# Values spread over partition groups by SBUF-to-SBUF DMA, Q and K transposed straight from staging, attention steps regrouped by PE tile mode

## The chip, the cores and the metric

The kernel runs on one core of one Trainium2 chip. The metric is device time in microseconds (us) of one execution. Most executions of one kernel lie within about 1 %; some fall into a slower state, with a lower granted TensorE clock. A ratio is the mean time of one kernel's fast runs over the mean time of the other's fast runs of the same rounds, so it is not quite the ratio of the medians that are quoted beside it.

Engines are named as the profile names them: PE is TensorE (matmul), DVE is VectorE, ACT is ScalarE, POOL is GpSimd, SP is SyncE, which issues DMAs. SBUF is the memory on the chip that the engines work on, HBM the large memory beside it. The *mode* of a matmul is the shape in which it uses TensorE's array; the profile prints it in each line (64\*128, 128\*128, 128\*64).

## The reference

Block-sparse attention (4 batches, 8 heads, 768 rows, 64 columns per head), followed by a two-layer network with exact GELU over the 3072 rows of 512.

```python
block, n_blocks, n_rand = 32, 24, 3
mask  = |block(i) - block(j)| <= 1                   # own block and both neighbours
mask |= block(i) in (0, 23) or block(j) in (0, 23)   # the first and last block, as rows and as columns
mask |= block(j) in sampled_blocks[block(i)]         # three drawn blocks for each query block
attn = softmax(where(mask, q @ k.T / sqrt(64), -1e9))
x = (attn @ v), heads side by side: [3072, 512]
out = gelu(x @ w_in) @ w_out                         # w_in [512, 2048], w_out [2048, 512]
```

Three kinds of score blocks follow from the mask. A query tile of 128 rows has "own" keys (itself and its neighbours, masked after the exponential), "global" keys (blocks 0 and 23) and "sampled" keys (four slots of 32: three drawn blocks and one more, gathered by GpSimd). The query rows of blocks 0 and 23 see every key: these are the "dense" steps.

## The kernel before

A batch is handled in two halves of 384 rows, a half in four head pairs. For each half there is a *hidden stage* (the `w_in` matmuls and GELU, with the next half's transposes and gathers filled in between) and then an *attention stage* (the next half's attention, with the `w_out` matmuls of this half filled in between). TensorE runs everything in program order.

```python
# Values: cast, to HBM, and back 16 times, so that partition group s holds the blocks rotated by s
def prep_v(b, v_st):
    dve.tensor_copy(v_pj, v_st.rearrange("p h (j d) -> p j h d", d=D))
    sp.dma_start(out=v_dram[b]..., in_=v_pj...)
def spread_v(b):
    for c in range(4):
        for s in range(4):
            i = 6 * ((c - s) % 4)
            sp.dma_start(out=v_rep[32 * s:32 * s + 32, i:i + 6, :], in_=v_dram[b]...[c])
def natural_v(b, eng):            # copies for the own and the global keys; ScalarE for batch 0
    copy(v_nat[b % 2][:, :, :, 0:D], v_rep[:, 0:NT, :]...)
    ...
# Q and K: a permuted copy, six transposes, one eviction
def transpose_qk(b, hp, which, pair, eng, st):
    pm = permute(pair, eng)       # one copy of 128x768, on VectorE in batches 1 to 3
    ps = mm_pool.tile([P, NT, P], BF16, tag="mm", name="ps")
    for j in range(NT):
        pe.transpose(ps[:, j, :], pm[:, j, :, :].rearrange("p h d -> p (h d)"), ident)
    dve.tensor_copy(dst..., ps...)
# Scores: two steps per pair, each with 64-row matmuls followed by 128-row ones
def scores_own(b, hb, hp, st):
    for m in range(MH):
        for h in range(2):
            pe.matmul(s1[:, h, ...], lhsT=kt[64 h : 64 h + 64, c], rhs=qt[64 h : 64 h + 64, c])
    for m in range(2):
        pe.matmul(s1[:, m, HALF:HALF + P], lhsT=gl, rhs=qt[:, ...])
    act.activation(pt[:, 0], s1, AF.Exp, scale=scale)
def scores_sampled(b, hb, hp, st):
    ... 22 matmuls of 64x32 from kg, then 2 of 128x64 from gl, then one Exp
...
def attention_steps(b, hb, st): ...   # own, sampled, late weighted, dense, ...
merge(attention_steps(...), output_steps(...))   # spreads the output pairs evenly between the steps
```

Every operation goes through one helper that keeps program order, so nearly all instructions carry its line (L52 before, L54 after); the lines of the profile are told apart by their tiles. Names: `s`, `sd` are scores, `pt`, `pd` their exponentials, `og`, `od` weighted sums, `psx`, `xT` the transposed attention output, `hp` the hidden layer, `g` its GELU, `op` the output layer, `tq`, `tk` transposed Q and K, `kg`, `v_gat` gathered keys and values.

The softmax here doesn't subtract the row's maximum and nothing guards it: scores larger than these inputs give would overflow.

## Time and profile before

The time before was 368.53 us (median of 3 runs, 367.51 to 368.89). The profile that came with it fell into a slow run (377.65 us). The kernel was profiled once more beside the experiments (369.58 us, mean granted clock 0.976; a single run, so of unknown state, but at the time of the fast ones). That profile is used below. These are its span, the busy time of TensorE and TensorE's busy tenths in 40 slices:

```profile
span 367.8 us, 8258 instructions
...
PE 280.2 (76%) x3632; PEld 159.7 (43%) x3632; DVE 158.3 (43%) x358; ACT 153.0 (42%) x173; POOL 107.9 (29%) x119
...
PE   0340038899977759886996999867978898999995
```

Each digit stands for 9.2 us. The first seven are a start in which TensorE mostly waits; after that it is busy, with dips. TensorE's waits from its first `w_in` matmul (69.4 us) to the end, from the list of waits (total us, times, longest):

```profile
PE ps L52 <- DVE pm L52: 21.3, 20, 2.6
PE og L52 <- POOL v_gat L52: 4.1, 2, 2.5
PE sd L52 <- ACT pt L52: 3.9, 3, 1.3
PE hp L52 <- DVE xT L52: 3.6, 4, 1.1
PE s L52 <- ACT pt L52: 3.0, 4, 0.9
PE psx L52 <- DVE x L52: 0.9, 4, 0.2
```

They sum to 36.8 us (0.7 of it in front of that first matmul), and 21.3 of them are for the permuted copy `pm`. In the timeline of TensorE (start, duration, what, and the idle time before it) this looks so:

```profile
105.94 0.51 PE L52 MATMUL ps<-ident,pm 128*128 128x128 bf16 x6 [1.91 <-DVE pm L52]
106.29 1.46 PE L52 MATMUL hp<-xT,w_in_sb 128*128 128x384 bf16 x8
108.04 0.51 PE L52 MATMUL ps<-ident,pm 128*128 128x128 bf16 x6 [0.29 <-DVE pm L52]
```

One set of six transposes takes 0.35 us (105.94 to 106.29), but TensorE waits before it. The start is bound by the values. In the timeline of ScalarE, the copy of the values stands in front of the first exponential and waits for the DMAs back from HBM; in that of TensorE, the first dense scores wait for that exponential:

```profile
44.06 2.75 ACT L52 COPY v_nat<-v_rep 128x3072 bf16<-128x3072 bf16 x1 [20.61 <-DMA v_rep<-v_dram]
```

```profile
49.50 0.50 PE L52 MATMUL sd<-tq,tk 64*128 64x64 bf16 x12 [22.56 <-ACT pt L52]
...
54.80 0.41 PE L52 MATMUL og<-v_gat,pt 128*32 128x65 bf16 x14 [2.06 <-POOL v_gat L52]
...
69.37 1.12 PE L52 MATMUL hp<-xT,w_in_sb 128*128 128x384 bf16 x3 [0.73 <-DVE xT L52]
```

The last line is where the start ends. I cut the span there, and after that at each change between hidden and attention work in TensorE's timeline:

| part of the span (us) | before |
|---|---|
| start, to the first `w_in` matmul | 69.4 |
| 8 hidden stages | 120.4, of which waits 21.3 |
| 7 attention stages with output matmuls | 163.7, of which waits 14.8 |
| last output stage | 14.4 |
| span | 367.8 |

### The profile page before, as it was taken

To read this page: it belongs to the slowest core of one execution; us is meant where nothing else is said; L and a number is where in the kernel's file an instruction comes from. 1 tells how busy PE (TensorE), PEld (TensorE's weight loads), DVE (VectorE), ACT (ScalarE), POOL (GpSimd) and SP (SyncE) were. 2 spreads that over 40 slices of the span, in tenths; PEclk is the share of its full clock that TensorE was granted. 3 is DMA by queue.
4 is the path that set the end of the run, shared out by engine and by line. 5 is a ranking of instruction groups with operands and counts; after the bars stand their busy time and mean duration, and the time that the engine had idled before them with its cause. 6 is when DMAs were issued, how large, how long until landed. Compare 5 with 4: busy or idle time off the path is not lost. (4 is left out here: it accounts for less than half of the span.)

```text
span 375.9 us, 8258 instructions
## 1 busy us (share of the span) xinstructions
PE 284.4 (76%) x3632; PEld 161.5 (43%) x3632; DVE 164.7 (44%) x358; ACT 153.3 (41%) x173; POOL 108.4 (29%) x119
## 2 busy tenths in 40 slices
PE   0340058699966859786896989876997899999995
PEld 0230046454543425443453545543554455545552
DVE  4298035513467625726446255535564045014201
ACT  2410366066321714223650575244523843475330
POOL 8331467430012374320244553100342531000000
PEclk9999999599998979969999999999999999999999
DMA  5979909978900029359201490179010000001102
GB/s 186 241 187 258 197 7 186 203 157 184 222 30 2 0 36 214 81 171 211 50 30 58 61 192 32 77 197 202 32 38 20 2 30 31 30 2 41 46 0 84
DMA packets 34419, 37.82 MB, mean 101 GB/s; under 512 B 2000, under 2 KB 30800, under 8 KB 34384
## 3 DMA queue, kind: packets, MB, share of 16 engines
q1 hardware_dynamic: 18576, 23.67, 24.0%
q0 software_dynamic: 14720, 12.06, 20.7%
q10 hardware_dynamic: 1088, 1.57, 1.1%
q8 instruction: 28, 0.46, 0.5%
q14 instruction: 7, 0.06, 0.1%
HBM read 39.92 MB, written 9.44 MB: 131 GB/s over the span
## 5 line engine op out<-in xcount | busy, mean ns | idle before, releaser
L52 PE MATMUL op<-w_out_sb,g 128*128 128x512 bf16 x384 | 106.7, 385 | 0.0
L52 ACT ACTIVATE g<-hp 128x768 bf16<-128x768 f32 x64 | 51.9, 811 | 123.5 <-PE hp L52 123.5
L52 PE MATMUL hp<-xT,w_in_sb 128*128 128x384 bf16 x512 | 92.7, 340 | 7.5 <-DVE xT L52 7.5
L52 POOL INDIRECT_COPY kg<-tk,idx_k 128x704 f32 x32 | 40.8, 1276 | 109.4 <-issue 72.6
L52 PEld LDWEIGHTS <-w_in_sb 128*128 128x128 bf16 x512 | 51.3, 102 | 43.3 <-issue 13.9
L52 DVE TENSOR_TENSOR pt<-pt,mask_x 128x768 bf16<-128x768 bf16 x32 | 28.8, 899 | 85.0 <-ACT pt L52 85.0
L52 PE MATMUL ps<-ident,pm 128*128 128x128 bf16 x192 | 18.8, 245 | 41.1 <-DVE pm L52 21.8
L52 POOL INDIRECT_COPY v_gat_201<-v_rep,idx_v 128x1024 f32 (+1 forms) x12 | 19.7, 1640 | 69.1 <-issue 35.6
L52 PEld LDWEIGHTS <-g 128*128 128x128 bf16 x384 | 29.2, 98 | 16.9
L52 PEld LDWEIGHTS <-pm 128*128 128x128 bf16 x192 | 13.4, 109 | 49.6 <-DVE pm L52 28.6
L52 PEld LDWEIGHTS <-pt 128*32 128x32 bf16 (+2 forms) x1024 | 26.2, 100 | 18.5 <-issue 6.8
L52 PEld LDWEIGHTS <-tk 64*128 64x128 bf16 x384 | 10.7, 100 | 46.3 <-issue 45.6
L52 DVE COPY os<-op 128x512 f32<-128x512 f32 x24 | 16.5, 688 | 23.2 <-PE op L52 23.1
L52 POOL INDIRECT_COPY v_gat_202<-v_rep,idx_v 128x1024 f32 (+1 forms) x12 | 19.6, 1636 | 21.4 <-issue 8.7
L52 PE MATMUL sd<-tq,tk 64*128 64x64 bf16 x192 | 6.2, 202 | 25.8 <-ACT pt L52 25.8
L52 DVE COPY tk<-ps 128x768 bf16<-128x768 bf16 x16 | 15.3, 956 | 23.7 <-PE ps L52 23.7
L52 ACT ACT_TABLE_LOAD x16 | 20.5, 1283 | 6.7 <-issue 4.8
L52 ACT ACTIVATE pd<-sd 128x768 bf16<-128x768 f32 x16 | 13.0, 813 | 19.4 <-PE sd L52 19.4
L52 DVE COPY tq<-ps 128x768 bf16<-128x768 bf16 x16 | 15.3, 958 | 7.4 <-PE ps L52 7.2
L52 DVE TENSOR_TENSOR x<-og,rc 128x384 bf16<-128x384 f32 x32 | 17.8, 557 | 1.1
L52 DVE RECIPROCAL rc<-og 128x6 f32<-128x6 f32 x32 | 6.2, 194 | 25.1 <-PE og L52 25.0
L52 PEld LDWEIGHTS <-kg 64*128 64x128 bf16 x704 | 11.2, 94 | 12.9 <-issue 10.3
(321 smaller groups left out, 304.7 us busy)
## 6 DMA issues: line engine op xcount, KB each, us to landing
out_dram<-os SPq DMA_DIRECT2D x24, 256.0 KB, 2.0
st_v<-in_v_dram POOLq DMA_DIRECT2D x4, 768.0 KB, 15.2
v_rep<-v_dram_205 SPq DMA_DIRECT2D x16, 192.0 KB, 8.5
v_rep<-v_dram_206 SPq DMA_DIRECT2D x16, 192.0 KB, 6.5
v_rep<-v_dram_207 SPq DMA_DIRECT2D x16, 192.0 KB, 7.0
v_rep<-v_dram_208 SPq DMA_DIRECT2D x16, 192.0 KB, 6.1
st<-in_k_dram POOLq DMA_DIRECT2D x6, 384.0 KB, 7.3
st<-in_q_dram POOLq DMA_DIRECT2D x6, 384.0 KB, 9.5
```

The costliest lines, as they stand in the source:

```text
L52: return self._tc.keep_in_program_order(f(*args, **kwargs))
```

## The change

Its intent is to take work and waits off TensorE's path, in three parts:

1. **Values.** They are read in their natural layout as float32 (runs of 256 bytes), cast once into a buffer `v_flat`, and rotated over the four groups of 32 partitions by six SBUF-to-SBUF DMAs. The trip through HBM, the copy to `v_nat` and the waiting ScalarE copy are gone.
2. **Transposes.** The permuted copy `pm` is gone. Each head is transposed from the staging tile itself (in batch 0 from a plain bf16 cast of it): 12 transposes of 64 columns, in column-tiled mode, instead of 6 of 128.
3. **Attention by tile mode.** The 64-row score matmuls of a pair (own and sampled) run as one group and the 128-row ones after them. The dense steps use zero-padded 128x128 operands (`qgl`), so they too run in the full mode. Output matmuls come in larger blocks, with the counts written into the schedule.

It also reorders the start: index arithmetic is shared between VectorE and GpSimd, and the memsets move to VectorE.

```diff
 # values
-    def prep_v / spread_v / natural_v ...
+    def own_v(b, st_v, i, eng):
+        cast(eng, v_own[b % 2][:, 3 * i:3 * i + 3, :, 0:D], st_v[:, 3 * i:3 * i + 3])
+    def rotate_v(b, r):
+        for lo, hi, src in ((0, P - 32 * r, 32 * r), (P - 32 * r, P, 0)):
+            sp.dma_start(out=v_all[lo:hi, NT * r:NT * r + NT], in_=v_own[b % 2][src:src + hi - lo])
+    def global_v(b, s, eng): ...          # four small copies to vgl, from the rotated groups
 # transposes
-        pm = permute(pair, eng)
...
-            pe.transpose(ps[:, j, :], pm[:, j, :, :].rearrange("p h d -> p (h d)"), ident)
+            for h in range(2):
+                pe.transpose(ps[64 * h:64 * h + 64, j, :], pair[:, h, j * D:j * D + D], ident)
 # scores: both buffers at once, by mode
+        s1 = sc_pool.tile(...)
+        s2 = sc_pool.tile(...)
+        ... 6 own and 22 sampled matmuls of 64 rows, then
+        for m, o in enumerate((s1[:, 0, HALF:HALF + P], s1[:, 1, HALF:HALF + P], s2[:, 0, NR_Q:NR_Q + P])):
+            pe.matmul(o, lhsT=gl, rhs=qt[:, q0 + m * P:q0 + m * P + P], start=True, stop=True)
+        ... three activations instead of two
 # schedule: (step, output parts after it)
+            steps = [(S_(0), 3), (D_(0), 2)]
+            for hp in range(1, NPAIR):
+                steps += [(S_(hp), 0), (E_(hp - 1), 0), (W_(hp - 1), 2), (D_(hp), 2)]
...
 # start
     for hp in range(NPAIR):
         ...
         if hp == 0:
+            load_w_in(0)
+            value_columns()
+            value_indices(0, dve)
+            mark_valid(0)
+            clear_rest()                  # VectorE memsets
+        elif hp == 1:
+            load_w_in(1)
+            own_v(0, first_v, 0, dve)
+            own_v(0, first_v, 1, act)
+            for r in range(1, 4):
+                rotate_v(0, r)
+    for s in range(4):
+        global_v(0, s, dve)
+    for c in range(len(VCH)):
+        gather_v(0, 0, c)
...
+    value_indices(1, pool)
```

## The prediction

> **What bounds the kernel now.** Two stages. (1) Start: in the timeline TensorE has its first w_in matmul only at 71.7 us. It waits there for Values: they go to HBM (issued 19.4 us) and come back as 16 spread DMAs (issued 22.7 to 35.0); ScalarE, in program order, waits 20.0 us for them (list of waits) before its first exponential at 47.8, and the first weighted sum ends after the third gather, at about 54.5. (2) From 71.7 on TensorE is the limit: the sum over windows has it busy 252 of the last 296 us. Its idle time there is mostly waits in the stages with Q/K transposes: the list of waits has 21.8 us on the permuted copy `pm` (19 waits, longest 2.9), about 8 on evictions, 6.2 on gathered values, 4 on exponentials. The profiled run was a slow one (377.65 against a median of 368.53; windows show granted clock 0.74 to 0.93 between 60 and 180 us), so I cost in differences.
>
> **Mode changes.** "TensorEngine Tiling (Array Packing)", Key Properties, says that changing the tiling mode drains the array. The trace agrees: two output matmuls take 0.43 us when the next is of the same mode, 0.53 when it is not, so about 0.10 us per change.
>
> **Costs per head pair, from starts in the timeline at full clock, switches included.** Own plus sampled scores 1.04 us now; 6 + 22 in one mode, then 3 global: estimate 0.80. Weighted sum 0.86, without the 128x64 part 0.75. Dense scores 0.38 -> 0.34; dense weighted 0.60 -> 0.34. First halves gain 4 x 0.65, second halves 4 x 0.35. Over the seven halves beside output matmuls about 14 us, all on TensorE, so critical.
>
> **Transposes.** Without the permute the 21.8 us of `pm` waits go. They become 12 transposes of 64 columns in a 128x64 mode instead of 6 of 128: if the two column halves overlap, 24 cost 0.7 + 0.2 us; if not, about 1.5. Before 0.68. Loss 2 to 10 us over 12 pairs, I take 5. VectorE has two evictions of 0.96 us per pair left, so some waits return; two pairs stand back to back in batches 1 and 2. I estimate 38 us of idle becoming 14.
>
> **Start.** First loads of 4.7 MB landed at 18 us. Values are now read as 256-byte runs; "DMA: Bandwidth & Descriptors", Specifications, wants 512 B for line rate (no run here shows that yet). Estimate: Values land at 20 to 24 us, last Q/K at 25 to 28, rotation (2.4 MB, 6336 B pieces, 8 us at the 235 ns per 6144 B seen) at about 34, three gathers at 3.5 us to 45. ScalarE no longer waits, so scores of pairs 0 and 1 are done by then. First w_in matmul at about 60 instead of 72: gain 12 us, uncertain by 6.
>
> **Sum.** -14 (modes) + 5 (transposes) - 24 (waits) - 12 (start) = -45: **322 us**, 8 in 10 between 308 and 342. Faster by over 2%: 0.93; within 2%: 0.05; slower: 0.02.
>
> **What would show it.** `pm` waits gone, waits of `ps` under 10 us; TensorE idle after the first w_in matmul under 20 us; first w_in matmul at 55 to 65 us; ScalarE's long wait for `v_rep` gone; 24 transposes within 1.0 us; output pairs at 0.43 more often; dense weighted 0.34.
>
> **What would make it wrong.** 256-byte value loads or rotation far slower than estimated, so the start gains nothing (+10); column-tiled transposes that do not overlap (+5); TensorE waiting for exponentials since both score buffers are taken at once (third exponential per pair), or for VectorE with the f32 casts; output stores stuck behind value loads on the same queue; GpSimd copies slowing VectorE.

## More of the kernel before

A wait is counted in the stage in which it falls. The waits for `xT` in front of the first `w_in` matmul of later hidden stages (2.8 us) therefore belong to the attention stages. The text on record for experiment 4 counts them with the hidden stages: its 12.0 us of attention waits before should be 14.8.

## The result, and the profile after

The changed kernel took 349.81 us (median of 4 runs, 346.8 to 350.82) against 368.71 us for the kernel before (4 runs, one of them, 375.75, far above the others). The ratio of the fast runs is 0.948 [0.940, 0.956]: faster by 5 %. The direction was right. The time was not: 349.81 lies outside 308 to 342, and 28 us above 322. (The terms of the prediction sum to -45, which taken from 368.53 is 323.5; the 322 was rounded with no reason.)

The profile after is of a fast run (mean granted clock 0.99):

```profile
span 349.0 us, 8094 instructions
...
PE 265.5 (76%) x3532; PEld 165.3 (47%) x3568; DVE 134.6 (39%) x333; ACT 154.8 (44%) x205; POOL 115.4 (33%) x171
...
PE   1216103779889878897879989888989898989995
```

TensorE is busy for 14.7 us less, of which some 8 us (an estimate: 36 missing records of output matmuls, 0.216 us from start to start) are only missing from the trace, and it is still busy for only 76 % of the span. The list of its waits from the first `w_in` matmul (74.9 us) on; the lines left out are the one for output matmuls after "issue", five more of the kind of the last one, and smaller ones:

```profile
PE psx L54 <- DVE xT L54: 5.8, 7, 1.9
...
PE s_1613 L54 <- POOL kg L54: 2.8, 1, 2.8
PE sd L54 <- ACT pt L54: 2.2, 2, 1.1
PE psx L54 <- DVE xdT L54: 2.1, 3, 0.7
PE ps L54 <- DVE tk L54: 1.6, 2, 0.8
PE hp L54 <- DVE xT L54: 1.3, 1, 1.3
PE hp L54 <- ACT g L54: 0.9, 1, 0.9
PE ps L54 <- DVE tq L54: 0.7, 2, 0.3
PE s_2230 L54 <- ACT g L54: 0.6, 1, 0.6
```

All waits on `pm` are gone, and in their place stand new, small ones of several kinds: for `xT`, for `g`, for `xdT`, for gathered keys. The waits on "issue" (about 4 us on `op`) are left out of every sum here: they are gaps where records of matmuls are missing (348 of 384 output matmuls are in this trace).

The transposes, in the timeline of TensorE, where the lines of before had a wait in front of most sets:

```profile
109.15 0.86 PE L54 MATMUL ps<-ident,st 128*64 128x128 bf16 x24
109.94 2.77 PE L54 MATMUL hp<-xT,w_in_sb 128*128 128x384 bf16 x16
```

Twenty-four transposes, a whole head pair, take 0.79 us from start to the next start, with no wait. The scores of one head pair, first before (two steps, each with a change of mode in it, and output matmuls between them) and then after (one step):

```profile
180.60 0.34 PE L52 MATMUL s<-tq,tk 64*128 64x128 bf16 x6
...
181.00 0.59 PE L52 MATMUL op<-w_out_sb,g 128*128 128x512 bf16 x2
181.53 0.44 PE L52 MATMUL s<-tq,kg 64*128 64x32 bf16 x22
...
181.97 1.03 PE L52 MATMUL op<-w_out_sb,g 128*128 128x512 bf16 x4
```

```profile
207.16 0.34 PE L54 MATMUL s_2952<-tq,tk 64*128 64x128 bf16 x6
...
207.88 0.51 PE L54 MATMUL od<-v_flat,pd 128*128 128x130 bf16 x6
```

They took 0.40 + 0.44 us before and take 0.72 now, and one change of mode less stands in front of them. The start, on the other hand, has become longer. TensorE's timeline there:

```profile
25.31 0.85 PE L54 MATMUL ps<-ident,bf_q_377 128*64 128x128 bf16 x12 [5.68 <-DVE tk L54]
...
42.38 0.48 PE L54 MATMUL og<-vgl_219,pt 128*128 128x130 bf16 x3 [7.58 <-DVE vgl_219 L54]
...
49.12 0.25 PE L54 MATMUL og<-v_gat_222,pt 128*32 128x65 bf16 x4 [5.63 <-POOL v_gat_222 L54]
...
55.53 0.41 PE L54 MATMUL og<-v_gat_222,pt 128*32 128x65 bf16 x14 [2.51 <-POOL v_gat_222 L54]
...
61.47 0.81 PE L54 MATMUL od<-v_flat,pd 128*128 128x130 bf16 x6 [2.97 <-DVE xd L54]
...
74.93 1.30 PE L54 MATMUL hp<-xT,w_in_sb 128*128 128x384 bf16 x7 [1.27 <-DVE xT L54]
```

The long wait for an exponential is gone, as intended; the gathered values now come last. The first weighted sum ends at about 55.9 us, no earlier than before (about 55.1), and from there to the first `w_in` matmul it takes 19.1 us instead of 14.2. What VectorE does meanwhile, from its timeline:

```profile
13.09 0.23 DVE L54 TENSOR_TENSOR colf<-colf,ok 128x66 f32<-128x66 f32 x1 [2.02 <-POOL ok L54]
...
17.82 1.83 DVE L54 MEMSET v_flat<- 128x1856 uint32 x3 [0.33 <-issue]
...
24.36 0.90 DVE L54 COPY tk<-ps 128x768 bf16<-128x768 bf16 x1
...
26.07 1.04 DVE L54 CAST v_flat<-st_v 128x1536 bf16<-128x1536 f32 x1
...
60.92 0.17 DVE L54 RECIPROCAL rc<-od 128x2 f32<-128x2 f32 x1 [17.54 <-POOL idx_v_164 L54]
```

VectorE runs in program order. It waits for GpSimd's `ok`, computes value indices until 17.5 us, and clears buffers until 24.4; only then does it evict `tk` of the second pair (for which TensorE waits 5.68 us) and cast its half of the values. ScalarE had found the values landed and cast its half at 16.5 us. The rotation, in the timeline of SyncE, follows VectorE's cast:

```profile
15.00 0.47 SPq L54 DMA_DIRECT2D first_q_108<-in_q_dram  x1
27.19 6.47 SPq L54 DMA_DIRECT2D v_flat<-v_flat  x6
```

Last, the line at 60.92: VectorE is idle for 17.54 us because its small tile `rc` is "released" by GpSimd's write of the *second* set of value indices (the one for batches 1 and 3). The two share no data. `rc` comes from a pool that reuses the memory of the start's tiles, and GpSimd, in program order, reads those tiles for the second indices only after its three gathers. That costs TensorE the 2.97 us at 61.47.

The stages before and after (profiles of 367.8 and 349.0 us):

| part of the span (us) | before | after | difference |
|---|---|---|---|
| start, to the first `w_in` matmul | 69.4 | 74.9 | +5.5 |
| 8 hidden stages | 120.4 (waits 21.3) | 98.9 (waits 3.2) | -21.5 |
| 7 attention stages | 163.7 (waits 14.8) | 160.7 (waits 20.6) | -3.0 |
| last output stage | 14.4 | 14.4 | 0 |

So the hidden stages gained nearly all that there was, the attention stages needed 8.8 us less of work and gave 5.9 us back in waits, and the start lost. Where did the expected 12 us of the start and most of the mode gain go?

### The profile page after: what moved, and what is told of

Its sections match the earlier page's. It is cut to its first block, busy times and chain, and to the rows that moved or that the text cites. A ratio compares the mean times of both kernels' runs of the same rounds, so it can differ in the third digit from the quotient of the medians.

```text
span 349.0 us, 8094 instructions
## 1 busy us (share of the span) xinstructions
PE 265.5 (76%) x3532; PEld 165.3 (47%) x3568; DVE 134.6 (39%) x333; ACT 154.8 (44%) x205; POOL 115.4 (33%) x171
## 5 line engine op out<-in xcount | busy, mean ns | idle before, releaser
L54 PE MATMUL op<-w_out_sb,g 128*128 128x512 bf16 x348 | 88.7, 387 | 4.6 <-issue 4.0
L54 PE MATMUL hp<-xT,w_in_sb 128*128 128x384 bf16 x512 | 86.8, 327 | 2.2 <-DVE xT L54 1.3
L54 DVE TENSOR_TENSOR pt<-pt,mask_x 128x768 bf16<-128x768 bf16 x32 | 22.9, 718 | 90.3 <-ACT pt L54 90.3
L54 PEld LDWEIGHTS <-pt 128*32 128x32 bf16 (+1 forms) x992 | 24.1, 100 | 23.4 <-issue 19.9
L54 DVE COPY os<-op 128x512 f32<-128x512 f32 x24 | 16.5, 686 | 23.4 <-PE op L54 23.4
L54 POOL INDIRECT_COPY v_gat_222<-v_flat,idx_v_164 128x1024 f32 (+1 forms) x6 | 9.5, 1587 | 41.6 <-DMA st_v<-in_v_dram 20.6
L54 PEld LDWEIGHTS <-tk 64*128 64x128 bf16 (+1 forms) x288 | 13.8, 102 | 20.1 <-issue 17.4
L54 POOL INDIRECT_COPY v_gat_222<-v_flat,idx_v_163 128x1024 f32 (+1 forms) x6 | 9.5, 1586 | 28.4 <-issue 17.9
L54 PE MATMUL psx<-ident,x 128*128 128x128 bf16 x96 | 9.8, 226 | 8.7 <-DVE xT L54 5.8
L54 PE MATMUL og<-v_gat_222,pt 128*32 128x65 bf16 x352 | 6.8, 207 | 11.6 <-POOL v_gat_222 L54 11.6
L54 PEld LDWEIGHTS <-x 128*128 128x128 bf16 x96 | 7.0, 101 | 14.2 <-issue 9.2
L54 POOL INDIRECT_COPY v_gat_223<-v_flat,idx_v_163 128x1024 f32 (+1 forms) x6 | 9.5, 1575 | 11.5 <-issue 9.2
L54 DVE COPY xT<-psx 128x512 bf16<-128x512 bf16 (+1 forms) x24 | 9.6, 402 | 9.4 <-PE psx L54 9.2
## 6 DMA issues: line engine op xcount, KB each, us to landing
st<-in_q_dram POOLq DMA_DIRECT2D x6, 384.0 KB, 10.2
```

The source lines that it names most:

```text
L54: return self._tc.keep_in_program_order(f(*args, **kwargs))
```

## The experiments

For the start, theory one was VectorE's program order: index arithmetic and memsets stand ahead of the eviction and the cast on which the rotation waits. Theory two was the shared memory behind `rc`. The rival of both was that the rotation itself is slow, by its nature or by contention with the weight loads, so that issuing it earlier would gain little; or that the value loads in 256-byte runs are the limit. For the rest, the theory (called M in places) was that the regrouping does save its 14 us of TensorE time, and that new waits, which come from its order, give them back; its rivals were that fewer mode changes save little in the first place, and (N in the texts) that the regrouping alone is worth its 14 us and another part of the change took them back. The texts below were written before the runs; where they call a theory by a letter alone, it is one of these.

The kernel before was run and profiled once for comparison:

> No theory is told apart: the first profile of the kernel before fell in the slow state (377.65 us). This look should be a fast one, about 368 to 369 us, and give its stages at full clock: first w_in matmul near 71 us, about 297 us from there to the end. My prediction put the changed kernel at 60 + 262; its trace has 74.9 + 274.1, so the error is about 15 us in the start and 12 us in the rest, and this run should confirm that the start gained nothing.

It took 369.58 us (one run, state unknown); its profile is the one used above.

### Experiment 1: VectorE's start reordered

```diff
@@ start of the kernel after, at hp == 0
-            value_columns()
-            value_indices(0, dve)
-            mark_valid(0)
-            clear_rest()
+            clear_v()                     # only the memset that the values' buffer needs
@@ behind the loop over the four pairs
+    value_columns()
+    value_indices(0, dve)
+    mark_valid(0)
+    clear_rest()
```

> The changed kernel with VectorE's index arithmetic and its memsets (13.1 to 24.4 us of the trace) moved behind the evictions and the cast of Values. Theory A: the start is late because VectorE, in program order, casts the Values only at 26.1 us although they had landed by about 16 us, so the rotation is issued at 27.2; then the rotation starts at about 18 us, everything after it is 8 to 10 us earlier, first w_in matmul at 65 to 67 us, time 340 to 342. Rival B: the value loads in 256-byte runs are the limit; then the rotation starts at the same 27 us and the time stays within 2 us of 350. Rival C: the rotation itself (27 to 46 us) is the limit by its queue and begins earlier but ends hardly earlier; gain under 4 us.

Measured: 341.4 us (340.96 to 341.79), ratio to before 0.925 [0.921, 0.929]. The rotation was issued at 18.4 us instead of 27.2, and the first `w_in` matmul came at 66.5 instead of 74.9. In the timelines of SyncE and TensorE:

```profile
18.42 7.41 SPq L54 DMA_DIRECT2D v_flat<-v_flat  x6
```

```profile
66.55 4.72 PE L54 MATMUL hp<-xT,w_in_sb 128*128 128x384 bf16 x16 [1.59 <-DVE xT L54]
```

The order of VectorE's work was worth 8 us of the time. Theory one holds, and the value loads were not the limit.

### Experiment 2: the second set of value indices before the gathers

```diff
+    value_indices(1, pool)
     for c in range(len(VCH)):
         gather_v(0, 0, c)
...
     mark_valid(1)
-    value_indices(1, pool)
     first_ctx.close()
```

> The changed kernel with the second set of value indices on GpSimd emitted before the gathers instead of after them. Theory D: the first reciprocal of the attention waits until 60.9 us because its tile lies in memory that the start's tiles free only when GpSimd has made the second indices (60.9 us), behind three gathers and two load issues; then the VectorE wait of 17.5 us ends at about 56, TensorE's 3.0 us wait of od for xd goes, first w_in matmul 3 to 5 us earlier, time 345 to 347. Rival E: that wait only covers another one (exponentials, evictions) and under 1.5 us is gained.

Measured: 347.28 us, ratio 0.942 [0.937, 0.946], against 0.948 of the kernel after; the two intervals overlap, so the time alone does not settle it. The trace does: TensorE's 2.97 us wait for `xd` is gone and the first `w_in` matmul comes at 71.3, 3.6 us earlier. Theory two is right and small.

### Experiment 3: both

```diff
-            value_columns() ... clear_rest()      # moved behind the loop, as in experiment 1
+            clear_v()
...
+    value_indices(1, pool)                        # before the gathers, as in experiment 2
...
-    value_indices(1, pool)
```

> Both edits. If theories A and D hold and are independent, the gains add: first w_in matmul at 60 to 63 us (my prediction said 60), time 336 to 338. If the index wait is hidden once the rotation is early, the gain is that of the first edit alone, 340 to 342.

Measured: 340.96 us (338.59 to 343.48), ratio 0.926 [0.920, 0.932]; first `w_in` matmul at 64.5. The start of the rotation in the timelines of SyncE and GpSimd:

```profile
17.87 5.43 SPq L54 DMA_DIRECT2D v_flat<-v_flat  x6
```

```profile
39.11 1.65 POOL L54 INDIRECT_COPY v_gat<-v_flat,idx_v 128x1024 f32 x1 [5.72 <-DMA st_v<-in_v_dram]
```

In the kernel after, GpSimd's line was:

```profile
47.41 1.66 POOL L54 INDIRECT_COPY v_gat_222<-v_flat,idx_v_163 128x1024 f32 x1 [10.47 <-DMA st_v<-in_v_dram]
```

(The releaser printed there is one of batch 1's value loads, which are issued behind the rotation and share its semaphores. In the program, the gather reads what the rotation writes, and it comes before those loads.) The rotation is issued 9.3 us earlier than in the kernel after, and the first gather starts 8.3 us earlier (47.41 to 39.11). But 21 us still lie between the issue and the first gather: 4.0 to the first packet, 12.9 for the rotation and 4.3 from its last packet to the gather. The prediction had given the rotation 8. In time, this version does not differ from experiment 1: the gains did not add up to the 336 to 338 us that the text hoped for. The wait for `xd`, still 2.97 us in experiment 1, is gone here and the start is 2 us shorter, but the runs spread over 5 us, so what the second edit adds to the first stays unsettled.

### Experiment 4: the regrouping alone, in the kernel before

The kernel before, with the new scores, dense steps, weighted sums and schedule, and nothing else. The copies of Q's global blocks (`qgl`) went to GpSimd.

```diff
-    def scores_own ... def scores_sampled ... def dense_scores ...
+    def scores ... def dense_scores ...      # as in the change
-    def attention_steps ...                  # and merge
+    def attention_steps ...                  # as in the change, with weave
+            (dve if which == "k" else pool).tensor_copy(gl_[rs, rs]..., dst[rs, :]...)
```

> The kernel before with only the attention steps regrouped by mode (scores in one step, dense steps over 128 columns, the new weave), Values and Q/K transposes as before. My prediction priced this at 14 us. Stages of the fast profiles: the seven stages of attention beside output matmuls take 163.7 us before and 160.7 in the changed kernel, only 2.9 less, although their TensorE idle fell out of the sum: 12.0 us of waits before, 20.6 after. Theory M: mode changes do cost what I said, and new waits (both score buffers taken at once, a transposed x behind another with no output matmul between them) give most of it back; then these stages are 3 to 6 us shorter in sum, their waits rise by 5 to 9 us, time 362 to 367. Rival N: the regrouping is worth its 14 us and something else of the change (Values on VectorE and DMA) took it back; then 353 to 357.

Measured: 384.44 us, ratio 1.039 [1.031, 1.046], slower. This spoke for neither theory, because the edit had a fault of its own, which the list of TensorE's waits shows:

```profile
PE s L52 <- POOL kg L52: 13.9, 2, 7.0
```

My `qgl` copies stood ahead of the gathers on GpSimd, and there they waited for transposes. It is a miss of mine and not a measure of the regrouping; experiment 7 mends it.

### Experiment 5: the direct transposes alone, in the kernel before

```diff
-        pm = permute(pair, eng)
+        pm = permute(pair, eng) if b == 0 else None
...
+            for h in range(2):
+                pe.transpose(ps[64 * h:64 * h + 64, j, :], pair[:, h, j * D:j * D + D], ident)
```

> The kernel before with only the transposes of batches 1 to 3 taken straight from staging (no permuted copy). My prediction priced this at -21.8 us of waits, +5 of TensorE time, and some waits of evictions coming back. The stages with transposes take 120.4 us before and 98.9 in the changed kernel. Theory: nearly all of the gain of the whole change is here; then these stages are 15 to 22 us shorter and the time is 347 to 354. Rival: they need the new pacing of the fills as well, because two transposes in a row wait for their evictions on VectorE; then under 10 us is gained, 359 or more.

Measured: two fast runs of 349.26 and 350.49 us and two slow ones of 356.21 and 356.9; the kernel before stood at 370.18 in the same rounds (7 fast runs, median). In the profile (a fast run, span 348.5) the hidden stages fell from 120.4 to 97.3 us, and in the list of waits nothing waits for `pm` any more; the attention stages stood at 166.7. In the fast runs that are there, this one part alone takes about as long as the whole change. It is an observation from two fast runs.

### Experiment 6: another order of the attention stages

The kernel after, with two output parts *before* the first scores of each stage (instead of all of them after), one or two output parts between the transposes of `x`, the copies of the global values moved to the next hidden stage, and the cast and rotation of the next values placed into the first 14 output parts.

```diff
-            steps = [(S_(0), 3), (D_(0), 2)]
+            steps = [(lambda: None, 2), (S_(0), 4), (D_(0), 2)]
...
-                + [lambda r=r: rotate_v(b, r) for r in range(1, 4)]
-                + [lambda s=s: global_v(b, s, dve) for s in range(4)])
+                + [lambda r=r: rotate_v(b, r) for r in range(1, 4)])    # global_v: in the hidden stage
...
-            groups = spread(fill, aux)
+            groups = spread(fill[:14], aux) + fill[14:]
```

> The changed kernel with other places for the output matmuls beside attention: two ahead of the first scores, more behind them, one or two between the transposes of x; and the copies of the global values moved out of VectorE's way into the next stage. If the 20.6 us of waits in the seven attention stages are what keeps the mode changes from paying, they fall to 6 to 10 us and the time to 337 to 341 (from about 349). If they only move to other places (score buffers, og buffers), under 4 us is gained.

Measured: 336.5 us (336.44 to 339.22), ratio 0.912 [0.906, 0.919]. No arithmetic was changed, and the attention stages fell from 160.7 to 147.1 us, their waits from 20.6 to 9.3. The first waits of the list, from the first `w_in` matmul on:

```profile
PE s L54 <- POOL kg L54: 4.0, 3, 2.5
PE op L54 <- issue: 3.3, 21, 0.2
PE hp L54 <- DVE xT L54: 1.9, 3, 0.9
```

The 5.8 us of `psx<-xT` and the six waits on `g` are gone. The latter came about because `scores` takes both score buffers at once, and the second of them is held by the last GELU of the hidden stage until it is through; two output parts (each a pair of matmuls, 0.43 us) ahead of the scores are enough to cover that. So the order of the steps was what had given most of the mode gain back in the changed kernel. The wait on gathered keys stayed (4.0 us).

### Experiment 7: the regrouping alone, mended

```diff
-            (dve if which == "k" else pool).tensor_copy(
+            dve.tensor_copy(
```

> r5 again, with the copies of the global queries on VectorE instead of GpSimd. r5 was slower by 14 us and spoke for neither theory: its trace shows 13.9 us of waits for gathered K because my copies on GpSimd waited there for the transposes, ahead of the value gathers in program order. Without that: theory M (new waits give most of the mode gain back) expects waits for gathered K under 3 us, the seven attention stages 1 to 6 us shorter than before, the transpose stages 2 to 4 us longer for the copies, time 363 to 370. Rival N (the regrouping is worth its 14 us alone) expects 354 to 358. If it is above 374, the regrouping needs the other parts of the change for a reason that I have not found.

Measured: 367.96 us (365.15 to 370.02), ratio 0.996 [0.988, 1.005]: the same as before. By stages (span 367.5): start 72.1, hidden 123.6, attention 157.5 with waits of 18.0, last 14.35. So TensorE's work in the attention stages fell by 9.4 us (163.7 - 14.8 before, 157.5 - 18.0 now), their waits rose by 3.2, the hidden stages lost 3.2 (waits on `pm` are 23.9 us instead of 21.3, with the copies to `qgl` now on VectorE too) and the start 2.7. The saving is real, so the rival that it is small falls, and so does N, which wanted 354 to 358 us. It is given back almost to the microsecond, but theory M, new waits from the order of the steps, accounts here for only a third of that. The waits that are new in the attention stages are also in the kernel after; from the list from the first `w_in` matmul on:

```profile
PE psx L52 <- DVE xT L52: 3.4, 7, 0.5
...
PE s L52 <- ACT g L52: 3.1, 5, 0.6
```

### Experiment 8: everything together

Experiments 1, 2 and 6 in one kernel, and in addition the gathered keys of batch 1's first pairs ahead of its gathered values.

```diff
         elif b == 0:
-            aux = v_steps(1, 0)
+            aux = []
             for hp in range(NPAIR):
                 aux += t_steps(1, (hp,)) + k_steps(1, 0, (hp,))
+                if hp == 1:
+                    aux += v_steps(1, 0)
```

> The edits of r4 (VectorE order and early indices) and of r7, with the K gathers of batch 1 ahead of its value gathers on GpSimd. If start and rest are independent, the gains add: 341 less 9 to 13 and up to 3 for the gathers, 327 to 332.

Measured: 326.02 us (325.74 to 326.9), ratio 0.882 [0.877, 0.887]. It beats both kernels; against the changed one the medians, which are of different rounds, differ by 24 us. By stages (span 324.4): start 64.7, hidden 98.6, attention 146.7, last 14.4. The gains of the start (from 73.8 in experiment 6 to 64.7) and of the attention stages add up.

### Experiment 9: is the rotation slow by itself?

Experiment 8, with the loads of the first two parts of `w_in` issued after the gathers, so that no weight load runs beside the rotation.

```diff
-            load_w_in(0)
...
-            load_w_in(1)
...
-    for c in range(2, 4):
+    for c in range(4):
         load_w_in(c)
```

> r8 with the first two w_in loads moved behind the first gathers, so that nothing else moves while the Values are rotated between partition groups at the start. In all runs so far a packet of the rotation (6336 B, SBUF to SBUF) takes about 400 ns, also in batches 1 to 3 where no other packets are between them, and one rotation 11.4 to 12 us; in the start of r4 it takes 12.9 us and begins only when the last Q/K loads are through. Theory: the rotation is slow by itself; then its packets stay at 390 to 410 ns, it takes 11.5 us instead of 12.9, the first gather starts 1 to 4 us earlier and the time is 323 to 326, if w_in then lands in time. Rival: contention with w_in is what makes it slow; then packets fall to about 240 ns, it takes 7 us, the first gather starts 6 us or more earlier and the time is 319 to 322.

Measured: 325.33 us (324.38 to 326.49), ratio 0.881 [0.875, 0.887], no different from experiment 8. From the DMA records of the traces, the 384 packets of 6336 bytes of the first rotation:

| | first start to last end | median packet |
|---|---|---|
| kernel after, at the start | 28.4 to 44.2 us: 15.7 | 435 ns |
| kernel after, batches 1 to 3 | 11.7, 11.6, 11.4 | 400 to 403 ns |
| experiment 3, at the start | 21.9 to 34.8: 12.9 | 392 ns |
| experiment 8, at the start | 20.4 to 35.4: 15.0 | 408 ns |
| this one, at the start | 19.0 to 32.8: 13.8 | 444 ns |

The rotation did not fall to the 8 us of the prediction, nor its packets to the 235 ns that the kernel before shows for 6144 bytes from SBUF to HBM, although the weight loads were out of its way. With the loads beside it, it had taken 12.9 to 15.7 us, so these loads made no clear difference and are not by themselves the main cause. But the rotation was not alone in this run, whatever its label says: batch 1's value loads, issued behind it on the same queue, took the place of the weights (1496 packets of 256 bytes beside it instead of 282 in experiment 8). The DMA records add up simply. Divided by 16 engines, the rotation's packets took 10.2 us at the start of the kernel after and all others in that stretch 6.7, in experiment 3 9.4 and 4.7, and here 10.8 and 4.1: each sum is within 1.2 us of the whole stretch, so the engines were busy all through it. In batches 1 to 3 of the kernel after, 9.4 us of rotation packets and about 1.8 of others (output stores, which the text overlooks) make the 11.4 to 11.7. So the slow packets are there with little beside them, and what shares the engines adds 4 to 7 us at the start. A start without the value loads beside the rotation was not tried. The start ended at 61.1 instead of 64.7, but the keys for batch 1 then came later (4.3 us of TensorE waits on `kg` instead of 3.2, and the attention stages took 149.3 instead of 146.7), and the time stayed the same.

## Why the prediction was right or wrong

The sum of the prediction, term by term, against the two profiles:

| term | predicted (us) | measured (us) |
|---|---|---|
| modes | -14 | about -10.5 |
| transposes themselves | +5 | about +2 |
| waits after the start | -24 | -12.2 (hidden -18.1, attention +5.9) |
| start | -12 | +5.5 |
| the rest, not predicted | 0 | about -4 |
| sum | -45 | about -19 |

The spans themselves differ by 18.8 us. The rest is not taken apart by any run. Two things in the trace before belong to it: the clock records show half the clock from 114.8 to 118.2 us, where eight `w_in` matmuls took 2.56 us instead of 1.30, and in two more stretches after the start (to 73.8, and 131.9 to 138.7; the kernel after has two such stretches of 3.4 us); and a set of transposes that is followed by a wait took 0.50 us besides the idle time (from 103.53 us on), where one without took 0.35.

**Modes: right in kind, some 3 us too high.** Where no stretch at half the clock falls, the attention stages' time less their waits fell by 2.2 us in each first half and 1.0 in each second half, where 2.6 and 1.4 were predicted: 10.5 us for the seven. Experiment 7 confirms it from the other side with 9.4. "TensorEngine Tiling (Array Packing)" of the Trainium skill, Key Properties, says that a switch of the mode drains the engine; the 0.10 us per switch that the prediction read from the trace is there in both traces (an output matmul is followed after 0.31 us by one of another mode, after 0.22 by one of its own). No run takes apart how much of the saving comes from fewer switches and how much from fewer matmuls.

**Transposes: the loss was at the low end.** The prediction took a loss of 5 us from 2 to 10. A pair's 24 column-tiled transposes took 0.79 us and the switch in front of them about 0.1, and two sets of six full ones took about 0.70 before: some 0.2 us per pair, or 2 us for 12 pairs (an estimate from these times). That is the prediction's case of two column halves that run side by side (0.7 + 0.2); that they do is not shown by itself. The same page of the Trainium skill lists, under Restrictions and Gotchas, that column tiling excludes Fast Weight Load; no cost of that is seen here.

**Waits: the step "38 us idle becoming 14" failed.** The first half of it was right: `pm` is gone, and waits in the hidden stages fell from 21.3 to 3.2, with `ps` at 2.3 us where under 10 were predicted. In the two fast runs of experiment 5 this was about the whole gain of the change. The other half was not: the attention stages gained 5.9 us of waits. The prediction named "both score buffers are taken at once" as a risk and put no time to it; that one took six times 0.6 us on `g`. It named waits for VectorE only "with the f32 casts", and had no thought for `psx` waiting on VectorE's evictions (5.8 us on `xT` and 2.1 on `xdT`), with a single wait of 1.94 where VectorE stood behind a copy to `vgl` that was itself waiting 2.00 us for the rotation. Late gathered keys took another 3.7, after 4.1 us on gathered values before. Idle time after the start was predicted under 20 us, and was 23.8 without "issue". Experiment 6 removes 11 us of the attention stages' waits by order alone.

**Start: the step that failed most was "rotation (2.4 MB, 6336 B pieces, 8 us at the 235 ns per 6144 B seen) at about 34".** The 235 ns belonged to a copy from SBUF to HBM, and I carried them over to a copy within SBUF, where packets of nearly the same size take 390 to 440 ns (median). The rotation took 15.7 us and ended at 44.2. Two things made it long: its 384 packets took 10.2 us on each of 16 DMA engines, where 235 ns each would give 5.6, and other transfers (batch 1's value loads and a weight load) took 6.7 us of the same engines, of which the prediction does not speak. The late end is 10 of the 15 us between the predicted 60 and the measured 74.9; the gathers after it took 11.7 us against 11. The rest lies behind them: 19.1 us instead of 15 to the first `w_in` matmul, of which 2.97 are the wait on shared memory. Part of what remains may be the array's rate: six own-score matmuls took 0.50 us until 59 us in the kernel before and 0.34 from 60.2 on, and in the kernel after still 0.50 at 64.1. That is argued, not tested. The prediction did name "rotation far slower than estimated, so the start gains nothing (+10)" as a risk; the whole miss of the start is 17.5.

The start of the rotation was nearly right (26 follows from the prediction's 34 less 8; 28.4 measured), by two errors that cancel. The value loads in 256-byte runs were *not* slow: ScalarE had them at 16.5 us, where 20 to 24 were predicted. And VectorE's cast came 10 us after the landing, because I had assumed that values are cast as soon as they land and had not followed VectorE's program order. Experiment 1 shows what that order cost: with the rotation issued at 18.4 us the kernel is at 341.4, just inside the predicted range.

Experiment 8 reaches 326.0 us with no less arithmetic. A gain of the predicted size was therefore there to be had; the changed kernel lost more than half of it through the order of its own new work.

**The signs that it named.** Right: `pm` gone, `ps` under 10 us, ScalarE's wait for the values gone, 24 transposes within 1.0 us, dense weighted sums at 0.34 (129.29 to 129.63 us in the timeline), output matmuls in blocks of one mode. Wrong: idle under 20 us, and the first `w_in` matmul at 55 to 65.

What stays open: why packets within SBUF take 1.7 times as long as those to HBM (experiment 9 rules out the weight loads as the main cause, and shows no cause), how much the start would gain without the value loads beside the rotation, and how the column-tiled transposes come to be so quick.

## What to carry to other kernels

When a change moves work to another engine, follow that engine's program order through the start: a memset or an index computation that "costs nothing" delays whatever stands behind it, and a copy that waits for a DMA blocks an engine for everyone. A step that groups work by mode takes more buffers at once, so put independent matmuls ahead of it and between its evictions, or the waits eat the gain. And take a DMA's duration from a DMA between the same two memories.

## What the Trainium skill lacked or had wrong

- "TensorEngine Tiling (Array Packing)", Key Properties, says that a mode switch drains TensorE and gives no size. Here it is about 0.10 us (a pair of output matmuls takes 0.43 us before one of the same mode and 0.53 before one of another), and the regrouping as a whole took about 9 to 10 us of work off TensorE.
- The same page, Restrictions and Gotchas, lists what column tiling excludes, but not what two column halves of a transpose cost beside one full one: 24 transposes of 64 columns took 0.79 us (and about 0.1 for the switch in front), against about 0.70 for 12 full ones.
- "DMA: Bandwidth & Descriptors", Specifications, asks for at least 512 bytes per piece for line rate. In the trace, 256-byte packets took 18 ns (median, 14 bytes per ns) and 1536-byte packets 65 ns (24 bytes per ns), so small ones ran at some 60 % of the rate; it did not limit the start.
- The same page says in "Why small descriptors are slow (HBM only)" that SBUF-to-SBUF transfers escape the penalty of small pieces. Small pieces within SBUF are not tested here, but for large ones the traces show copies within SBUF as the slower ones: 6336 bytes within SBUF took 392 to 444 ns (median) and 6144 bytes from SBUF to HBM 235. No page that I read gives a size for this.
- "TensorE: Matmul & The Clock Gate", Part 1, says that an idle array runs at half rate. The traces agree: eight `w_in` matmuls took 2.56 us from start to start at 115.6 us of the kernel before, where the clock record says 0.50, and 1.30 at 102.2; six dense score matmuls took 0.80 us at 31.5 us of the changed kernel and 0.50 us at 131 us. The page warns that the clock's trace events can be unreliable, but not of this case: the profile's granted clock shows 1.00 for that start, since the first record of the clock in that trace comes only at 73 us.
- No page that I read covers waits that arise when a pool reuses the memory of another pool's tiles: here a wait of VectorE ended only with it, after 17.5 us of idle time, and TensorE waited 2.97 us for it.
